# Converting the 64-bit weights of the second stage while attention runs, keeping the parts in device memory, and loading them later

## The chip, the cores and the metric

One core of one Trainium2 chip. The metric is the device time in microseconds of one execution of the whole program; lower is better. Engines are named as the profile names them: PE (TensorE), DVE (VectorE), ACT (ScalarE), POOL (GpSimd), SP (the queue that issues every DMA here).

## The reference

Three blocks in a row, each on 4 batches of 576 positions. The weights named in the kernel are `moe_w_in`, `moe_w_sg`, `moe_w_out` (first block after attention) and `moe2_w_theta`, `moe2_w_tok_r`, `moe2_w_tok_i`, `moe2_w_ch` (second block); those that are 64-bit floats come to the core as pairs of 32-bit words.

```python
# attention, 8 heads of 64 columns
scores = q @ k.T / 8 + min(-(cum_i - cum_j), 0), causal        # cum: running sum of max(s, 0)
x = softmax(scores) @ v                                        # heads side by side: 576 x 512
# first block
h = gelu(x @ w_in);  u, v = h[:, :512], h[:, 512:]
v_s = w_sg @ (layernorm(v) * g_ln) + b_sg
x = x + (u * v_s) @ w_out
# second block
theta = x @ w_theta
y = w_tok_r @ (x * cos(theta)) + w_tok_i @ (x * sin(theta))
u = x + y
out = u + max(u @ w_ch, 0)
```

## The kernel before, in words

The program is written in Python as one stream of instructions with priorities; a scheduler places each engine's instructions in an order that is fixed when the program is built. Each engine then works in that order and waits where an operand is late.

Every large product is made from operands split in two parts, a rounded one (`h`, high) and the remainder (`l`, low), with three products for each pair (high by high, high by low, low by high). A 64-bit weight is split by `split64` (L446): one ACT instruction scales the exponent word (L459, into the tile `wta`), three DVE instructions put the bits of a 32-bit float together (L460, L461, L463, on `wta` and the raw words `wraw`), an ACT cast makes the high part (L82) and a POOL subtraction the low part (L90). The same helper lines L82 and L90 serve all roundings and subtractions, and L93 all products.

The stages, in the order in which they finish:

1. Attention over 32 heads, `attention` (L411). One step g computes the scores of head g (tiles `sc`; DVE maximum L289, ACT exponential L290 into `E`), the transposes of head g-1 (L335, copied into `E0` and `Ef`), and at every second step the products `Y` with the values for a pair of heads (`pv_units`). `split_head` (L243) prepares head g+2: `qA` on POOL (L251) and DVE (L253), `kA` on ACT, `kB` on POOL, then three DMAs into `qB` and `kB`. `load_head` loads head g+4. The string `ORDER` (12 letters) or `ORDER_V` (15 letters) says in which order these pieces of a step are written.
2. Beside attention, from head 8 on, the first block of the batch just finished is fed in as filling for PE: `ffn_in` (products `fo`) and `ffn_gate` (products `fo`, result `uT`, stored as `gd`). Its 64-bit weight `w_in` is split there too (tile `wtab`), and `w_sg` is split from 32-bit floats.
3. The middle, after the last head: `ffn_in` and `ffn_gate` of batch 3; `wout` for the four batches (loads `gr` and `xr`, splits `gr` into `gh` and `gl`, products `wo`, sum `xr` at L691, store `x2d`); `theta` of batch 0 (load `x2T`, products `th`, sine and cosine). In this stage `second_weights` (L907) loads and converts `w_out`, `w_theta`, the nine slabs of `w_tok_r`/`w_tok_i` and `w_ch`: 21 slabs of 128 rows, each in two halves by `weights64` (L894), 42 pieces of 128 x 256 or 128 x 288. The call `self.later(prep)` writes one piece after every eighth unit of `ffn_in` and one after every unit of `wout`. Their raw tiles have three buffers (L899, L900).
4. The end: `mix` for batches 0 to 3 (products `yo` with `wkh`/`wkl`, products `co` with `wch`/`wcl`), with `theta` of the next batch as filling.

The tiles of the split weights (`woh`, `wol`, `wth`, `wtl`, `wkh`, `wkl`) lie where attention's tiles lay, so nothing can be written to them before attention is over. All DMAs go through the one SP queue, in order.

## Time and profile before

| | |
|---|---|
| median of 3 runs (lowest, highest) | 713.51 us (711.18 to 716.57) |
| time of the profiled execution | 712.53 us |
| its span, first to last instruction | 710.7 us |
| busy: PE, DVE, ACT, POOL | 666.2, 479.1, 378.5, 234.1 us |

Busy time is the time in which an engine has at least one instruction under way. Products overlap one another on PE, and their ends are modelled, so a PE that shows as busy is not at its peak rate; how many products pass in a stretch says more. The granted clock is a share of full speed.

Stages of the span as read from the first and last instructions of each: the first eight heads until about 69 us, heads with the first block as filling until about 363 us, the middle from 363 us until about 512 us, the end until 710.7 us.

### The profile page before, as it was taken

The numbers are of one execution on the slowest core, as the hardware profiler recorded it, in microseconds if no ns is written. First come the engines' busy times: TensorE is split into PE (matmuls) and PEld (weight loads), VectorE is DVE, ScalarE is ACT, GpSimd is POOL, SyncE is SP. The second block draws the span as 40 slices with busy tenths as digits, with TensorE's granted clock in tenths as the row PEclk, the third lists the DMA queues.
The fourth block names the chain that finished last, engine by engine and source line by source line (L and its number), as shares of the span: only waits on it lengthen the run. The fifth ranks groups of instructions, "written<-read, shape, count | busy, mean of one in ns | idle before, by whom it ended". The sixth has DMA issues, their size and how long they took to land.

```text
span 710.7 us, 12461 instructions
## 1 busy us (share of the span) xinstructions
PE 666.2 (94%) x4496; PEld 586.9 (83%) x4496; DVE 479.1 (67%) x918; ACT 378.5 (53%) x888; POOL 234.1 (33%) x257
## 2 busy tenths in 40 slices
PE   4999889999999999999999777998999999999998
PEld 3777658778979888888878667887999989989997
DVE  4788787854558565585458998898876368367522
ACT  1767556884476754668426534674744256056100
POOL 4466353464425553164237563423000100010000
PEclk9999989999999999999999899999999999999999
DMA  5665757223332344220142689973000300300101
GB/s 133 195 187 175 222 158 214 78 73 120 115 81 84 100 136 128 73 79 29 48 154 89 202 250 300 318 248 114 34 1 19 117 1 1 134 1 1 67 1 66
DMA packets 50092, 80.75 MB, mean 114 GB/s; under 512 B 7248, under 2 KB 18768, under 8 KB 50032
## 3 DMA queue, kind: packets, MB, share of 16 engines
q1 hardware_dynamic: 50032, 79.97, 36.5%
q8 instruction: 35, 0.57, 0.3%
q14 instruction: 25, 0.20, 0.1%
HBM read 56.19 MB, written 19.02 MB: 106 GB/s over the span
## 4 chain that ended last, share of the span: by engine, by line
PE 69%; DVE 9%; DMA 8%; ACT 5%; issue 3%; SPq 3%; POOL 2%; ACTq 0%; DVEq 0%; POOLq 0%
PE yo L93 16%; PE fo L93 14%; PE sc L93 8%; PE Y L93 7%; PE co L93 7%; PE th L93 6%; PE T L335 6%; PE wo L93 3%; DMA wraw<-in_moe_w_in 2%; DVE wta L461 1%; DMA gt<-in_moe_w_sg 1%; DMA x2T<-x2d 1%; ACT E L290 1%; PE tp L714 1%; DVE wta L463 1%
## 5 line engine op out<-in xcount | busy, mean ns | idle before, releaser
L290 ACT ACTIVATE E<-sc,negm 128x64 f32<-128x64 f32 (+4 forms) x160 | 84.1, 529 | 43.3 <-DVE negm L289 42.4
L289 DVE TENSOR_REDUCE negm<-sc 128x1 f32<-128x64 f32 (+4 forms) x160 | 73.8, 482 | 37.9 <-PE sc L93 36.7
L93 PE MATMUL yo<-wkh,zh 128*128 128x288 f32 x288 | 85.2, 296 | 0.1
L93 PE MATMUL yo<-wkh,zl 128*128 128x288 f32 x288 | 85.2, 297 | 0.0
L93 PE MATMUL yo<-wkl,zh 128*128 128x288 f32 x288 | 85.2, 296 | 0.0
L335 PE MATMUL T<-ident,E 128*128 128x128 f32 (+1 forms) x480 | 70.7, 278 | 1.9 <-ACT E L290 1.7
L93 PE MATMUL sc<-kA,qA 128*128 128x64 f32 (+3 forms) x192 | 64.0, 343 | 5.8 <-ACT E L290 2.5
L93 PE MATMUL sc<-kB,qB 68*128 68x64 f32 (+3 forms) x192 | 60.6, 322 | 3.8 <-DMA qB<-cpos 3.2
L335 PEld LDWEIGHTS T<-ident,E 128*128 128x128 f32 (+1 forms) x480 | 52.8, 132 | 11.3 <-ACT E L290 3.5
L86 POOL TENSOR_SCALAR xt<-x2s 128x128 fp32r<-128x128 f32 x16 | 10.9, 696 | 144.7 <-DVE x2s L90 144.7
L93 PE MATMUL fo<-x,wih 128*128 128x288 f32 x256 | 57.5, 304 | 0.2 <-ACT wih L82 0.2
L90 POOL TENSOR_TENSOR kB<-K,kA 64x576 fp32r<-64x576 f32 x32 | 50.0, 1564 | 21.0 <-ACT kA L82 18.2
L93 PEld LDWEIGHTS yo<-wkh,zh 128*128 128x128 f32 x288 | 54.0, 188 | 0.7 <-DVE x2T L787 0.4
L93 PEld LDWEIGHTS yo<-wkl,zh 128*128 128x128 f32 x288 | 54.0, 188 | 0.3
L93 PEld LDWEIGHTS yo<-wkh,zl 128*128 128x128 f32 x288 | 54.0, 188 | 0.1
L93 PE MATMUL co<-u,wch 128*128 128x288 f32 x256 | 52.9, 295 | 0.0
L93 PE MATMUL wo<-gh,woh 128*128 128x288 f32 x128 | 38.8, 305 | 10.1 <-DVE xr L691 5.6
L93 PEld LDWEIGHTS sc<-kA,qA 128*128 128x128 f32 x192 | 37.7, 200 | 11.6 <-ACT E L290 2.8
L93 PE MATMUL fo<-wih,x 128*128 128x512 f32 x128 | 44.3, 406 | 2.1 <-ACT wih L82 1.4
L93 PE MATMUL Y<-Ef,vr 128*64 128x128 f32 (+3 forms) x256 | 46.0, 467 | 0.0
L251 POOL TENSOR_SCALAR qA<-Q 128x576 fp32r<-128x576 f32 x32 | 22.4, 699 | 69.1 <-PE sc L93 54.6
L93 PEld LDWEIGHTS fo<-x,wih 128*128 128x128 f32 x256 | 42.4, 188 | 1.8 <-issue 1.2
(172 smaller groups left out, 1897.5 us busy)
## 6 DMA issues: line engine op xcount, KB each, us to landing
Q<-in_q SPq DMA_DIRECT2D x64, 144.0 KB
K<-in_k SPq DMA_DIRECT2D x64, 144.0 KB
qB<-qA SPq DMA_DIRECT2D x32, 144.0 KB
xd<-xT SPq DMA_DIRECT2D x16, 288.0 KB
gd<-uT SPq DMA_DIRECT2D x16, 288.0 KB
gr<-gd SPq DMA_DIRECT2D x16, 288.0 KB
xr<-xd SPq DMA_DIRECT2D x16, 288.0 KB
x2d<-xr SPq DMA_DIRECT2D x16, 288.0 KB
```

Of the source, the lines that this page charges most:

```text
L86: nc.gpsimd.tensor_scalar(out, src, 1.0, 1.0, op0=ALU.mult, op1=ALU.mult)
L90: e.tensor_tensor(out, a, f32(hi), op=ALU.subtract)
L93: self.nc.tensor.matmul(out, lhsT, rhs, start=start, stop=stop)
L251: nc.gpsimd.tensor_scalar(qA, Q2, 0.125, 1.0, op0=ALU.mult, op1=ALU.mult)
L289: nc.vector.tensor_reduce(negm[0:rows, col:col + 1], o, axis=ax, op=ALU.max, negate=True)
L290: nc.scalar.activation(out, o, AF.Exp, bias=negm[0:rows, col:col + 1], accum_out=sm[0:rows, j, col:col + 1])
L335: nc.tensor.transpose(T[0:n, col:col + P], E[:, c:c + n], self.ident)
L461: nc.vector.scalar_tensor_tensor(ta.bitcast(U32), Hi, 0x80000000, ta.bitcast(U32), op0=ALU.bitwise_and, op1=ALU.bitwise_or)
L463: nc.vector.scalar_tensor_tensor(ta.bitcast(U32), L, 29, ta.bitcast(U32), op0=ALU.logical_shift_right, op1=ALU.bitwise_or)
L714: nc.tensor.transpose(tp[0:r, dt * P:(dt + 1) * P], x2T[:, dt, a:a + r], self.ident)
```

## The change

The 42 pieces are no longer converted in the middle. A new generator, `convert_second`, converts them two at a time during attention: six steps for each two pieces (exponents on ACT, bits on DVE, high part on ACT, low part on POOL, store; the second piece one step behind the first), and the loads of the next two pieces at the start of the six. One step is taken at every second letter of `ORDER` or `ORDER_V`, from g = 10 on (`g > H + 1`). The high and low parts are written over the raw words and stored in `wd`, a buffer in device memory of 21 x 2 x 128 x 576 floats: 84 stores. `second_weights` now only loads them, one slab (two DMAs) at each call: 42 loads, at the same places in the program as the conversions before. To make room, `E0` and `Ef` have three buffers in place of four. `split64` is cut into `exponents64` and `bits64` with the same instructions.

```diff
-        self.E0 = [self.a1.tile([P, S], F32, name=f"E0{i}") for i in range(4)]
+        self.E0 = [self.a1.tile([P, S], F32, name=f"E0{i}") for i in range(3)]
...
-        Ef = self.a2.tile([P, 1280], F32, name="Ef", tag="Ef", bufs=4)
+        Ef = self.a2.tile([P, 1280], F32, name="Ef", tag="Ef", bufs=3)
...
-            for o in self.ORDER_V if gp > 0 and gp % 2 else self.ORDER:
+            for i, o in enumerate(self.ORDER_V if gp > 0 and gp % 2 else self.ORDER):
+                if g > H + 1 and i % 2:
+                    self.later(self.conv)
...
+            self.wd = dr.tile([21, 2, P, S], F32, name="wd")
...
+            self.conv = self.convert_second()
...
                 self.attention()
+            for _ in self.conv:
+                pass
             att.close()
...
-                self.stg = self.pool(ws, "stg", side="right")
...
+    def convert_second(self):
...
+        def load(j):
+            if j < len(pieces):
+                k, i, src, c = pieces[j]
+                raw = self.f2.tile([P, 2 * c], U32, name="wraw2", tag="wraw2", bufs=4)
+                for r, w in src:
+                    nc.sync.dma_start(raw[r:r + w.shape[0]], w[:, 2 * i * c:2 * (i + 1) * c])
+                tiles[j] = raw, self.f2.tile([P, c], F32, name="wta", tag="wta", bufs=2)
+
+        def step(j, f):
...
+            if f == "exponents":
+                self.exponents64(words, ta)
+            elif f == "bits":
+                self.bits64(words, ta)
+            elif f == "high":
+                self.rnd("act", hi, ta)
+            elif f == "low":
+                self.sub("pool", lo, ta, hi)
+            else:
+                for part, t in enumerate((hi, lo)):
+                    nc.sync.dma_start(self.wd[k, part, :, i * c:(i + 1) * c], f32(t))
+                del tiles[j]
...
+        steps = ("exponents", "bits", "high", "low", "store")
+        for j in range(0, len(pieces), 2):
+            load(j + 2)
+            load(j + 3)
+            for n in range(6):
+                if n:
+                    step(j + 1, steps[n - 1])
+                if n < 5:
+                    step(j, steps[n])
+                yield
...
     def second_weights(self):
...
+            for t in range(m):
+                for part, q in enumerate("hl"):
+                    nc.sync.dma_start(f32(getattr(self, name + q)[:, t]), self.wd[k, part, :, 0:n])
+                k += 1
+                yield
```

What this does to the order of the engines, at three places.

DVE in attention, from the preparation of one head (L253, the twentieth of 32) to that of the next. Before, only attention's own instructions stand there:

```order
L253 SCALAR_TENSOR_TENSOR qA<-Q_1939,qA 64x576
L309 TENSOR_SCALAR sm_85<-sm_85 128x10
L341 COPY Ef<-T 128x512
L310 RECIPROCAL r_86<-sm_85 128x10
L289 TENSOR_REDUCE negm_78<-sc 128x1 x2
L289 TENSOR_REDUCE negm_78<-sc_2376 128x1
L289 TENSOR_REDUCE negm_78<-sc 128x1
L337 COPY E_75<-T 64x512
L289 TENSOR_REDUCE negm_78<-sc 128x1
L253 SCALAR_TENSOR_TENSOR qA<-Q_2058,qA 64x576
```

Now, from the twentieth L253 on (L471, L472 and L474 are the three bit instructions, L460, L461 and L463 before; `wta` is the piece):

```order
L253 SCALAR_TENSOR_TENSOR qA<-Q_2076,qA 64x576
L471 TENSOR_SCALAR wta<-wta 128x288
L472 SCALAR_TENSOR_TENSOR wta<-wraw_2615,wta 128x288
L341 COPY Ef<-T 128x512
L474 SCALAR_TENSOR_TENSOR wta<-wraw_2615,wta 128x288
L309 TENSOR_SCALAR sm_85<-sm_85 128x10
L310 RECIPROCAL r_86<-sm_85 128x10
L289 TENSOR_REDUCE negm_78<-sc 128x1 x2
L471 TENSOR_SCALAR wta<-wta 128x288
L472 SCALAR_TENSOR_TENSOR wta<-wraw_2618,wta 128x288
L474 SCALAR_TENSOR_TENSOR wta<-wraw_2618,wta 128x288
L289 TENSOR_REDUCE negm_78<-sc_2577 128x1
```

Two pieces, six instructions, stand between this L253 and the third maximum. In all, 60 of the 126 bit instructions (20 pieces) stand before the twentieth L253 and 66 (22 pieces) after it, the last ahead of the twenty-eighth.

SP at the start of the middle (`gr` is the first thing that `wout` needs). Before, from the last loads of `w_out` on:

```order
L902 DMA wraw<-in_moe_w_out 128x512 x4
L902 DMA wraw<-in_moe_w_theta 128x512 x8
L902 DMA wraw<-in_moe_w_tok_r 128x576 x2
L674 DMA gr<-gd 128x576 x2
L902 DMA wraw<-in_moe_w_tok_i 128x576
L683 DMA xr<-xd 128x576 x2
L902 DMA wraw<-in_moe_w_tok_i 128x576
```

Now, at the end of the loads of the split slabs:

```order
L981 DMA wkh<-wd 128x576
L981 DMA wkl<-wd 128x576
L683 DMA gr<-gd 128x576 x2
L692 DMA xr<-xd 128x576 x3
L683 DMA gr<-gd 128x576
L675 DMA gd<-uT 128x576
```

The first `gr` stood behind 18 loads of raw pieces, which share three raw buffers; now it stands behind the 34 loads of split slabs of `w_out`, `w_theta` and `w_tok`, which wait for attention's tiles alone. The eight loads of `w_ch` come later.

DVE in the middle, around the second split of `gr` (`gl`). Before:

```order
L460 TENSOR_SCALAR wta<-wta 128x288
L461 SCALAR_TENSOR_TENSOR wta<-wraw,wta 128x288
L463 SCALAR_TENSOR_TENSOR wta<-wraw,wta 128x288
L662 SCALAR_TENSOR_TENSOR gt<-fo,gcol,bsg 128x288
L460 TENSOR_SCALAR wta<-wta 128x288
L461 SCALAR_TENSOR_TENSOR wta<-wraw,wta 128x288
L90 TENSOR_TENSOR gl<-gr,gh 128x576
L463 SCALAR_TENSOR_TENSOR wta<-wraw,wta 128x288
L662 SCALAR_TENSOR_TENSOR gt<-fo,gcol,bsg 128x288
L90 TENSOR_TENSOR gl<-gr,gh 128x576
```

Now, from the first `gl`:

```order
L671 SCALAR_TENSOR_TENSOR gt<-fo,gcol,bsg 128x288 x2
L90 TENSOR_TENSOR gl<-gr,gh 128x576 x2
L671 SCALAR_TENSOR_TENSOR gt<-fo,gcol,bsg 128x288
L90 TENSOR_TENSOR gl<-gr,gh 128x576
L671 SCALAR_TENSOR_TENSOR gt<-fo,gcol,bsg 128x288
L90 TENSOR_TENSOR gl<-gr,gh 128x576
L671 SCALAR_TENSOR_TENSOR gt<-fo,gcol,bsg 128x288
L90 TENSOR_TENSOR gl<-gr,gh 128x576
L700 TENSOR_TENSOR xr<-wo,xr 128x288 x2
L671 SCALAR_TENSOR_TENSOR gt<-fo,gcol,bsg 128x288
```

No piece is left on DVE between the gate (`gt`), the split of `gr` and the sum `xr`.

## Rows read from the trace of the kernel before

**Rows 1.** Page, part 2: busy tenths of 40 slices, 17.8 us each.

```profile
PE   4999889999999999999999777998999999999998
...
DVE  4788787854558565585458998898876368367522
```

**Rows 2.** Busy time by stage, instructions in brackets (windows of the span).

```profile
core 0: us, PE busy (x) PEld busy (x) DVE busy (x) ACT busy (x) POOL busy (x), PEclk, DMA share, GB/s
69.00:188.00 119.00, 110.51 (x707) 87.92 (x706) 82.61 (x150) 75.90 (x194) 56.44 (x55) 0.94 0.49 142
188.00:280.00 92.00, 91.97 (x641) 77.81 (x640) 57.12 (x107) 57.12 (x147) 40.35 (x45) 1.00 0.37 109
363.00:390.00 27.00, 25.70 (x152) 23.05 (x152) 22.56 (x55) 13.66 (x31) 17.50 (x20) 1.00 0.34 108
390.00:512.00 122.00, 104.13 (x660) 95.52 (x661) 107.38 (x209) 69.97 (x143) 47.32 (x52) 0.97 0.66 215
400.00:420.00 20.00, 17.60 (x118) 16.21 (x116) 19.27 (x34) 9.12 (x20) 12.50 (x13) 0.96 0.87 277
```

**Rows 3.** Chain that ended last, by line: 69-188 us, then 188-280 us.

```profile
by line: PE fo L93 19.5%; PE Y L93 12.4%; DMA wraw<-in_moe_w_in 10.4%; DMA gt<-in_moe_w_sg 8.0%; PE sc L93 6.5%; PE T L335 5.2%; ACT E L290 4.5%; issue 3.8%; DVE qA L253 2.7%; DVE negm L289 2.0%; ACT uT L640 1.8%; ACT wtab L459 1.7%; DVE wt
...
by line: PE fo L93 47.3%; PE sc L93 19.4%; PE Y L93 15.7%; PE T L335 15.2%; PE R L359 1.9%; PE sc L359 0.6%; issue 0.0%
```

**Rows 4.** Chain that ended last, middle: start, length, what.

```profile
443.23 8.80 DMA x2T<-x2d
...
455.86 0.87 PE tp L714 x8
...
498.38 3.18 PE wo L93 x24
501.56 2.73 PE th L93 x12
```

**Rows 5.** Groups of PE, 390-512 us: busy, mean | idle before.

```profile
L93 PE MATMUL wo<-gh,woh 128*128 128x288 f32 x128 | 38.8, 305 | 10.1 <-DVE xr L691 5.6 <-ACT gh L82 4.4
...
L93 PE MATMUL th<-wth,x2s 128*128 128x512 f32 x64 | 21.4, 398 | 0.9 <-DVE an L744 0.8
L93 PE MATMUL th<-wtl,x2s 128*128 128x512 f32 (+1 forms) x36 | 13.9, 391 | 0.0
...
L714 PE MATMUL tp<-ident,x2T 128*128 128x128 f32 (+1 forms) x36 | 5.1, 272 | 0.0
```

**Rows 6.** Timeline of PE, the gate of batch 3 and the first `wo`.

```profile
398.08 0.50 PE L93 MATMUL fo<-wsrh,vh 128*128 128x288 f32 x1 [3.00 <-DVE vh L90]
...
404.93 0.40 PE L93 MATMUL wo<-gh,woh 128*128 128x288 f32 x1 [0.41 <-ACT gh L82]
```

**Rows 7.** Busy time of the instructions on `wta`, by stage: DVE, ACT, POOL.

```profile
363.00:390.00 27.00, 15.48 (x32) 7.10 (x18) 6.78 (x9) 1.00 0.34 108
390.00:512.00 122.00, 48.16 (x94) 26.39 (x64) 31.65 (x34) 0.97 0.66 215
```

**Rows 8.** Timeline of SP's queue: the first `gr`.

```profile
400.46 0.90 SPq L674 DMA_DIRECT2D gr<-gd  x2
```

**Rows 9.** Timeline of DVE: the twentieth and the twenty-eighth L253.

```profile
188.33 1.85 DVE L253 SCALAR_TENSOR_TENSOR qA<-Q,qA 64x576 fp32r<-64x576 f32 x1
...
280.06 1.91 DVE L253 SCALAR_TENSOR_TENSOR qA<-Q,qA 64x576 fp32r<-64x576 f32 x1
```

**Rows 10.** Tile `wta`: durations in ns, minimum/median/maximum.

```profile
L460 DVE TENSOR_SCALAR wta<-wta x42: 272/297/915, 362.1 to 477.7; 128x256 uint32<-128x256 uint32 x24, 128x288 uint32<-128x288 uint32 x18
L461 DVE SCALAR_TENSOR_TENSOR wta<-wraw,wta x42: 396/444/1045, 363.5 to 481.0; 128x256 uint32<-128x256 uint32 x24, 128x288 uint32<-128x288 uint32 x18
L463 DVE SCALAR_TENSOR_TENSOR wta<-wraw,wta x42: 385/450/1054, 365.0 to 485.5; 128x256 uint32<-128x256 uint32 x24, 128x288 uint32<-128x288 uint32 x18
...
L90 POOL TENSOR_TENSOR wkl<-wta,wkh x18: 802/838/1803, 404.9 to 459.7; 128x288 fp32r<-128x288 f32 x18
```

**Rows 11.** Tile `qA`: DVE's subtraction, minimum/median/maximum in ns.

```profile
L253 DVE SCALAR_TENSOR_TENSOR qA<-Q,qA x32: 754/756/1973, 6.1 to 324.2; 64x576 fp32r<-64x576 f32 x32
```

More of the change, by code (lines that the diff above doesn't have):

```diff
@@ L456, in split64, with exponents64, bits64 @@
             nc.sync.dma_start(raw[0:rows].rearrange("p n t -> p (n t)"), src)
[L457 to L459 removed]
+        raw, ta = raw[0:rows], ta[0:rows]
+        self.exponents64(raw, ta)
+        self.bits64(raw, ta)
+        self.rnd("act", his, ta)
+        self.sub(sub, lo, ta, his)
+    def exponents64(self, raw, ta):
+        self.nc.scalar.mul(ta, f32(raw[:, :, 1]), 2.0 ** -112)
+    def bits64(self, raw, ta):
+        nc = self.nc
+        L, Hi = raw[:, :, 0], raw[:, :, 1]
         nc.vector.tensor_scalar(ta.bitcast(U32), ta.bitcast(U32), 3, None, op0=ALU.logical_shift_left)
@@ L818, in run @@
             self.cd = dr.tile([32, 2, S], F32, name="cd")
+            self.wd = dr.tile([21, 2, P, S], F32, name="wd")
+            rows = [slice(t * P, (t + 1) * P) for t in range(4)]
+            self.second = [([(0, w[r])], DM) for w in (self.w_out, self.w_th) for r in rows]
+            self.second += [([(0, (self.w_tr, self.w_ti)[i % 2][rows[i // 2]])], S) for i in range(8)]
+            self.second += [([(0, self.w_tr[512:576]), (64, self.w_ti[512:576])], S)]
+            self.second += [([(0, self.w_ch[r])], DM) for r in rows]
             self.cp = self.pool(root, "const")
```

52 lines of the change are left out of this document (21 added, 31 removed).

## The prediction

> **What bounds the kernel now.** I read the slices of the page first [rows 1]: PE shows nine tenths or more nearly everywhere except in slices 5 and 6 and in slices 23 to 25. In the second of these stretches DVE shows eight or nine tenths, as it does on to slice 29. So the kernel has one stage, the middle, in which PE starves beside a full DVE.
>
> Then the stages [rows 2]. From 390 to 512 us DVE is busy for 107.4 of 122 us. From 69 to 188 us (A below) it has 82.6 of 119, from 188 to 280 us (B) 57.1 of 92. A and B together leave 71.3 us of DVE unused.
>
> Third, the chains [rows 3]. In B it is products and transposes and nothing else: PE works without a pause and DVE's gaps are gaps beside it. In A the loads of `w_in` (10.4%) and `w_sg` (8.0%) are on the chain, 22 of its 119 us; there both PE and DVE wait for other things.
>
> Fourth, how much PE time the middle needs. In rows without a stall 24 `wo` products pass in 3.18 us (0.1325 each), 12 `th` products in 2.73 us (0.2275), eight transposes in 0.87 us (0.109) [rows 4]. Of the 660 PE instructions from 390 to 512 us [rows 2], 100 are `th` and 36 are `tp` [rows 5]; nearly all of the other 524 have 288 columns. 524 x 0.1325 + 100 x 0.2275 + 36 x 0.109 = 69.4 + 22.8 + 3.9 = 96.1 us. The stage takes 122, so 25.9 us are lost. The visible waits are 3.0 us for a split of `vh` [rows 6] and 10.1 us for `xr` and `gh` [rows 5]; the rest is many short ones, and products at a lower clock after the waits (granted 0.97 over the stage).
>
> **What the change removes.** From the middle go the pieces' instructions. On `wta` DVE was busy 15.5 us from 363 to 390 us and 48.2 us from 390 to 512 us [rows 7], 63.6 us for the 42 pieces but for a few instructions just before 363: 1.51 us for each piece. Without them DVE has 59.2 of 122 us left after 390. The 48 us of PE's waits and DVE's work are not the same thing, so I count the gain on PE alone: 25.9 us less what stays.
>
> What is late next? The loads. The first `gr` was issued at 400.5 us [rows 8], behind raw pieces that wait for one another's buffers, and the first `wo` product ran at 404.9 us [rows 6]. Now 34 loads of 9.4 MB stand ahead of `gr`, with nothing to wait for but attention's tiles. From 390 to 512 us the transfers ran at 215 GB/s with a share of 0.66 [rows 2], so about 326 GB/s at full share (an estimate): 9.4 MB take 29 us. Begun at about 363 us they end at 392, `gr` lands some 2 to 3 us later, and the gate's 112 products (15 us) cover PE until then. If they ran at the 277 GB/s of 400 to 420 us [rows 2], it would be 34 us and still within the gate. Over the whole stage the same bytes move as before, less those loaded ahead.
>
> Something stays: the sine chain of `theta`, the trip of `x2d` through memory into `x2T` (8.8 us on the chain [rows 4]), the round of two `gr` buffers. The nearest row is the stage from 363 to 390 us, with products in plenty and few such trips: PE misses 1.3 of 27 us [rows 2], 5%. Its bounds for 122 us are 0 and all 25.9; I take 5%, 6 us. Gain: 25.9 - 6 = 20 us (bounds 0 and 26).
>
> **What it adds to attention.** 42 pieces: 126 instructions on DVE, 84 on ACT, 42 on POOL, 46 loads and 84 stores on SP. By the order of the instructions 20 pieces stand before the twentieth L253 and 22 between it and the twenty-eighth; these run at 188 and 280 us [rows 9], so 20 fall into A and 22 into B. No work on PE.
>
> DVE price of a piece: 0.297 + 0.444 + 0.450 = 1.19 us by the medians [rows 10], 1.51 us as the crowded middle shows it. POOL also grows in attention, so I take 1.51. That is 30.3 us into A's 36.4 us of gaps and 33.3 us into B's 34.9: it nearly fits, and an engine that works in a fixed order cannot use every gap. How full can it be? The stage from 390 to 512 us shows 88%, and its fullest stretch 96% (19.27 of 20 us, 400 to 420 us [rows 2]); I take 92%. Time for A and B with a piece at p us: (139.7 + 42p) / 0.92 against 211 us now. At p = 1.51 it is 220.9, so 10 us are lost (A 4, B 6); at p = 1.19 the sum is under 211 and nothing is lost. Bounds: 0, as B's chain holds nothing but PE, and all 63.6 us.
>
> ACT gains 33.5 us [rows 7] where it was busy 133 of 211 us [rows 2], POOL 38.4 on 96.8: both stay well under DVE, cost 0. If DVE were not full, ACT at 79% would be next.
>
> Transfers: 11.6 MB of raw words in and 11.6 MB of parts out, onto 26.9 MB in A and B. Scaled by bytes, the share goes from 0.49 and 0.37 to about 0.8 in both: not full, but each transfer stands behind more. In A that touches the 22 us of loads on the chain; bounds 0 and a third more, 7 us. I take 0, because DVE's new work falls into these very waits.
>
> SP: a store waits for ACT's and POOL's part of its piece, and behind it in the queue stand the three DMAs into `qB` and `kB` of the head after next, and behind those its scores. They are queued a whole head ahead, and the eight heads of B take 92 us [rows 9], over 11 us each; a late store costs nothing until it is that late. Three buffers for `E0` and `Ef`: the fourth head back has been multiplied a step earlier in the order; 0, or short waits if `Y` runs late.
>
> **Sum.** The profiled execution took 712.5 us, 1 us under the median of 713.5. 712.5 - 20 + 10 = 702.5; I forecast 703, 1.5% under that median. A measurement of this kernel can tell about 1% from no change, 7 us.
>
> **The rivals.**
>
> *Port collisions fill DVE (slower).* `qA` on DVE takes 0.754 us alone and up to 1.973 us [rows 11], and `wta` instructions of 0.45 us up to 1.05 us [rows 10]: beside a POOL instruction a DVE instruction can stand still. Each piece brings a POOL subtraction of 0.838 us [rows 10]. If it holds up one attention instruction for half its length or a little more, 0.46 us, a piece costs 1.97 us: A and B take (139.7 + 82.7) / 0.92 = 241.7, 30.7 us more, and the total is 712.5 - 20 + 30.7 = 723. It decides from p = 1.75 on, where the loss equals the gain of 20. For it: PE's chain needs DVE's maxima, and in the new order up to six bit instructions stand in a row before one. Against it: in B the products of the first block stand between a maximum and what needs it, and keep PE fed.
>
> The Trainium skill has a rule for this: "SBUF — State Buffer", section "Who interferes with whom", says that DVE shares one pair of ports with GpSimd under an exclusive lock, that a DVE instruction with two inputs in SBUF is blocked for as long as a GpSimd instruction reads there, and that a reduction is not. The stretched `qA` agrees. By that rule taken in full every subtraction blocks a DVE instruction to its end, which puts a piece at 1.51 + 0.84 = 2.35 us, the loss at 48 us and the total at 741; by the rows alone it is 703.
>
> *The middle is held by its trips through memory (no change).* With the conversions gone, `gr` with two buffers, `xr` with three, `x2d` out and `x2T` in could still keep PE waiting for half of the 25.9 us. Gain 13, loss 10: 709. For it: 8.8 us for `x2T` on the chain [rows 4] and a share of 0.87 from 400 to 420 us [rows 2]. Against it: the 7.4 MB of `w_tok` and `w_ch` mostly leave that stretch.
>
> *Attention hides everything (faster still).* B's chain is PE alone, A waits for loads; then the loss is 0 and the total 692.5. Against it: DVE would have to run at 96% for 211 us.
>
> That the change does not do what it says can be left out: the order has the last piece ahead of the twenty-eighth of 32 heads, and none in the middle.
>
> **How the numbers follow.** Forecast 0.37, collisions 0.27, trips through memory 0.21, all hidden 0.15. The forecast's own range is 697 to 710, from 0 to 7 us for the late loads of A and 4 us to either side for the stalls that stay. About 0.72 of it lies more than 1% under the median (below 706.4), which is 0.27; with 0.15 of the hidden case and 0.03 of the third that makes 0.45 for faster. Collisions give 0.25 slower, and 0.03 comes from the edges of the others: 0.28. The rest, 0.27, is no change. The range of 8 in 10 runs from 689 (near all hidden) to 727 (collisions with a few us to spare).
>
> **What would show it.** Right: PE's loss between the start of `ffn_in` of batch 3 and the first `yo` falls to 10 us or less, the first `gr` is issued and lands before the gate ends, no `wta` stands after attention; A and B together grow by about 10 us, with DVE at 90% or more and a `wta` at about 1.5 us a piece. Wrong: attention grows by 20 us or more, with maxima late behind bit instructions and POOL subtractions, or with `w_in` late behind the new transfers; or the middle keeps more than 12 us of waits, now for `gr`, `xr` or `x2T`.

## The result, and the profile after

The changed kernel takes 717.19 us (median of 12 runs, 715.38 to 719.12) against 713.55 us (12 runs, 711.18 to 716.57). The ratio is 1.0052, with a 95% interval of 1.0037 to 1.0066: slower by half a per cent, where 1.5% faster was forecast. The range held the time, the direction was wrong.

Three places cut the span into stages: the first product of `ffn_in` of batch 3, the first product of `mix` (`yo`), and the end.

| profiled execution, us | before | after | difference |
|---|---|---|---|
| span | 710.7 | 717.4 | +6.7 |
| attention with its filling, up to the first `fo<-wih` of batch 3 | 363.6 | 391.4 | +27.7 |
| the middle, from there to the first `yo` | 145.3 | 124.1 | -21.1 |
| the end | 201.8 | 201.9 | +0.1 |

The first rows of the middle and of the end, before and then after:

```profile
363.64 0.50 PE L93 MATMUL fo<-wih,x 128*128 128x512 f32 x1 [0.68 <-DVE gt L662]
...
508.90 0.29 PE L93 MATMUL yo<-wkh,zh 128*128 128x288 f32 x1
```

```profile
391.35 0.50 PE L93 MATMUL fo<-wih,x 128*128 128x512 f32 x1 [0.68 <-DVE gt L671]
...
515.47 0.30 PE L93 MATMUL yo<-wkh,zh 128*128 128x288 f32 x1
```

The middle did what was forecast (20 us), attention lost 27.7 us where 10 were forecast. Between the medians the difference is 3.6 us and not 6.7; if the middle and the end are as in the profiles, attention lost some 25 us by the medians.

The slices of the page after, as in [rows 1] (17.9 us each):

```profile
PE   5899898798998989999999999899999999999998
...
DVE  6688898879788978676643534478686277458522
```

DVE's eights and nines, before mostly in slices 22 to 29, now stand mostly in slices 3 to 16; PE no longer has a hollow in the middle, but a seven and six eights in its first half, where it had two eights before.

The stages after, as in [rows 2] (A ended at the twentieth L253, B at the twenty-eighth; 205 and 311 us now, 188 and 280 before):

```profile
core 0: us, PE busy (x) PEld busy (x) DVE busy (x) ACT busy (x) POOL busy (x), PEclk, DMA share, GB/s
71.00:205.00 134.00, 119.15 (x723) 94.56 (x723) 111.21 (x211) 88.46 (x231) 76.28 (x75) 0.91 0.69 209
205.00:311.00 106.00, 97.16 (x631) 79.59 (x630) 87.81 (x173) 73.19 (x195) 61.62 (x67) 0.97 0.68 204
...
391.00:415.00 24.00, 23.65 (x138) 21.16 (x139) 9.84 (x27) 8.84 (x17) 8.60 (x13) 1.00 1.04 382
415.00:520.00 105.00, 101.37 (x682) 94.84 (x682) 61.03 (x113) 44.25 (x74) 11.98 (x16) 1.00 0.58 191
```

A is 133.4 us long now, 119.4 before; B 106.3, 91.7 before. DVE is busy for 111.2 of 134 us and 87.8 of 106: 83% in both, not the 92% that the sum took. PE's granted clock is lower too, 0.91 and 0.97 where it was 0.94 and 1.00 [rows 2], and PE is busy for longer with about as many products (119.2 us for 723 in A, before 110.5 for 707): a part of the loss shows as slower products between waits. From 391 to 415 us the slabs come in at 382 GB/s, more than the 326 that I had worked out, and from 415 us on DVE has 61 of 105 us to do: PE is the bound there.

The chain of waits by line, 205 to 311 us and then 311 to 389 us (the first is B; compare [rows 3]):

```profile
by line: PE fo L93 10.7%; issue 9.9%; DMA wd<-wraw 5.6%; PE sc L93 5.5%; DVE qA L253 4.7%; DMA wraw<-in_moe_w_ch 4.5%; PE Y L93 3.6%; DVE negm L289 3.6%; PE T L335 3.5%; POOL vT L570 3.5%; DVE wta L474 3.1%; DVE stats L561 2.9%; DVE wta L47
...
by line: PE fo L93 43.4%; PE sc L93 17.8%; PE Y L93 17.6%; PE T L335 16.2%; PE R L359 2.2%; POOL uT L673 1.0%; DVE gt L671 0.7%; PE sc L359 0.6%; DVE xT L387 0.5%; issue 0.5%; DVEq L387 0.0%
```

In B the chain before was PE alone. Now PE's four products make a quarter of it, and the rest is a mixture: stores of parts, raw loads of `w_ch`, `qA`, maxima, the bit instructions. From 311 us on, where no piece is left, the chain is PE alone again.

The middle after: PE's timeline at the first `wo`, then the chain around `x2T` (compare [rows 4] and [rows 6]), then SP's queue around the first `gr` (compare [rows 8]).

```profile
423.45 0.29 PE L93 MATMUL wo<-gh,woh 128*128 128x288 f32 x1
```

```profile
442.05 3.56 DMA x2d<-xr
...
447.00 5.28 DMA x2d<-xr
452.71 8.60 DMA x2T<-x2d
```

```profile
410.88 0.32 SPq L981 DMA_DIRECT2D wkl<-wd  x1
417.15 1.39 SPq L683 DMA_DIRECT2D gr<-gd  x2
```

`x2d` and `x2T` are on the chain as before (8.60 us against 8.80). The first `gr` is issued 25.8 us after the start of the stage and the first `wo` runs 32.1 us after it; before, it was 41.3 us.

### The profile page after: what moved, and what is told of

Same layout as the page of the kernel before. It is cut to its first block, busy times and chain, and to the rows that moved or that the text cites. A ratio compares the mean times of both kernels' runs of the same rounds, so it can differ in the third digit from the quotient of the medians.

```text
span 717.4 us, 12719 instructions
## 1 busy us (share of the span) xinstructions
PE 674.4 (94%) x4496; PEld 594.1 (83%) x4496; DVE 478.5 (67%) x917; ACT 376.6 (52%) x888; POOL 228.8 (32%) x257
## 4 chain that ended last, share of the span: by engine, by line
PE 55%; DVE 4%; DMA 4%; ACT 2%; issue 2%; POOL 1%; SPq 1%; ACTq 0%; DVEq 0%
PE yo L93 16%; PE fo L93 12%; PE co L93 7%; PE th L93 7%; PE wo L93 5%; PE sc L93 3%; PE Y L93 2%; PE T L335 2%; DMA x2d<-xr 1%; DMA x2T<-x2d 1%; PE tp L723 1%; DMA wd<-wraw 1%; DVE qA L253 1%; DMA wraw<-in_moe_w_ch 1%; DVE negm L289 1%
## 5 line engine op out<-in xcount | busy, mean ns | idle before, releaser
L335 PE MATMUL T<-ident,E 128*128 128x128 f32 (+1 forms) x480 | 74.4, 287 | 10.2 <-ACT E L290 5.8
L93 PE MATMUL sc<-kA,qA 128*128 128x64 f32 (+4 forms) x192 | 65.6, 354 | 11.3 <-ACT E L290 5.5
L335 PEld LDWEIGHTS T<-ident,E 128*128 128x128 f32 (+1 forms) x480 | 54.6, 137 | 20.5 <-ACT E L290 7.1
L86 POOL TENSOR_SCALAR xt<-x2s 128x128 fp32r<-128x128 f32 x16 | 9.2, 588 | 183.7 <-DVE x2s L90 183.4
L93 PE MATMUL sc<-kB,qB 68*128 68x64 f32 (+3 forms) x192 | 62.7, 333 | 3.5 <-DMA qB<-cpos 2.7
L90 POOL TENSOR_TENSOR kB<-K,kA 64x576 fp32r<-64x576 f32 x32 | 48.2, 1506 | 21.5 <-ACT kA L82 19.6
L90 POOL TENSOR_TENSOR wraw<-wta,wraw 128x256 fp32r<-128x256 f32 (+1 forms) x42 | 36.6, 877 | 40.1 <-ACT wraw L82 26.2
L93 PE MATMUL fo<-wih,x 128*128 128x512 f32 x128 | 45.8, 418 | 1.0 <-DVE gt L671 0.7
L673 POOL TENSOR_TENSOR uT<-gt,uT 128x288 f32<-128x288 f32 x32 | 27.5, 861 | 56.2 <-DVE gt L671 43.0
L93 PEld LDWEIGHTS sc<-kB,qB 68*128 68x128 f32 x192 | 40.4, 211 | 4.8 <-issue 3.0
```

The lines of the kernel that those rows point to most:

```text
L86: nc.gpsimd.tensor_scalar(out, src, 1.0, 1.0, op0=ALU.mult, op1=ALU.mult)
L90: e.tensor_tensor(out, a, f32(hi), op=ALU.subtract)
L93: self.nc.tensor.matmul(out, lhsT, rhs, start=start, stop=stop)
L335: nc.tensor.transpose(T[0:n, col:col + P], E[:, c:c + n], self.ident)
L673: nc.gpsimd.tensor_tensor(uT[:, ft, a:a + m], gt, uT[:, ft, a:a + m], op=ALU.mult)
```

## The experiments

All times in the table are read in one way: the start of batch 3 and the length of the middle from the one profiled execution, the ratio to the kernel before from the timed runs. "Against three" is the start of batch 3 less 362.1 us, that of the kernel with three buffers alone. The changed kernel contains those buffers, so that kernel is the fair base for the conversion. But a single profile can lie some us from its kernel's median: the one of *three* took 704.97 us, 3.6 under its median of 708.53, the one of *lw400_17* 4.1 over. So the column "by medians" gives the same difference from the timed runs: the ratio less that of *three*, times 713.55 us, less the difference of all that comes from the start of batch 3 on, which is taken from the profiles (it differs by little between kernels: the end is 201.8 to 202.3 us in all but *lw100*, where it is 204.7). By the intervals of the ratios it is good to 2 to 4 us either way, in *noload_nosub* and *noload_nobits* to 4 to 5. Where the two columns differ, the medians are the better measure.

| kernel | start of batch 3 | against three | by medians | middle | median | ratio to before, interval |
|---|---|---|---|---|---|---|
| before | 363.6 | +1.5 | -0.7 | 145.3 | 713.55 | 1 |
| changed | 391.4 | +29.2 | +24.1 | 124.1 | 717.19 | 1.0052, 1.0037 to 1.0066 |
| three | 362.1 | 0 | 0 | 139.1 | 708.53 | 0.9925, 0.9900 to 0.9949 |
| e03 | 356.4 | -5.7 | -7.2 | 144.9 | 706.40 | 0.9904, 0.9871 to 0.9937 |
| dmaonly | 372.1 | +10.0 | +5.7 | 123.8 | 698.61 | 0.9788, 0.9758 to 0.9818 |
| dma_late | 360.0 | -2.1 | -5.6 | 124.2 | 688.92 | 0.9636, 0.9603 to 0.9670 |
| noload | 381.6 | +19.5 | +18.0 | 123.7 | 711.34 | 0.9964, 0.9942 to 0.9986 |
| noload_nosub | 372.6 | +10.5 | +9.2 | 123.7 | 702.81 | 0.9839, 0.9780 to 0.9899 |
| noload_nobits | 367.5 | +5.4 | +1.4 | 124.7 | 696.82 | 0.9748, 0.9691 to 0.9805 |
| nobits | 374.3 | +12.2 | +11.7 | 123.8 | 704.10 | 0.9875, 0.9845 to 0.9905 |
| nosub | 378.8 | +16.7 | +14.7 | 124.4 | 706.69 | 0.9923, 0.9905 to 0.9941 |
| five | 386.3 | +24.2 | +23.8 | 123.4 | 716.20 | 1.0038, 1.0007 to 1.0068 |
| lw100 | 384.6 | +22.5 | +17.7 | 121.8 | 712.53 | 0.9969, 0.9948 to 0.9990 |
| lw400 | 384.7 | +22.6 | +21.2 | 124.5 | 713.59 | 1.0016, 0.9979 to 1.0053 |
| lw400_17 | 385.4 | +23.3 | +16.5 | 128.2 | 713.37 | 1.0006, 0.9973 to 1.0039 |
| lw400_13 | 374.7 | +12.6 | +10.0 | 131.3 | 709.92 | 0.9955, 0.9924 to 0.9986 |
| s8 | 365.3 | +3.2 | +0.9 | 137.0 | 705.58 | 0.9907, 0.9878 to 0.9937 |
| s8b | 371.9 | +9.8 | +3.8 | 137.3 | 711.43 | 0.9950, 0.9923 to 0.9977 |
| s12 | 383.0 | +20.9 | +16.5 | 130.2 | 715.75 | 1.0029, 1.0009 to 1.0050 |
| s17 | 390.0 | +27.8 | +30.0 | 127.4 | 724.83 | 1.0184, 1.0137 to 1.0230 |

The middle is 123.4 to 124.7 us in every kernel with all 42 pieces in attention at the scheduler's old priorities: that term does not depend on how the pieces are made. All the rest is attention.

The ratios show the same ranking as the starts of batch 3 for the kernels that have all 42 pieces in attention.

### Which theories there were

L: ACT and DVE stand, in their fixed order, before pieces whose raw words are late. D: DVE's time for the bit instructions. C: POOL's subtractions hold DVE up. T: the new transfers make attention's own loads late. The first four kernels take one thing away each.

**nobits**: `self.bits64(words, ta)` replaced by `pass`.

> The changed kernel without the three DVE bit instructions of each piece (126 instructions; the parts that are stored and later multiplied are then not the weights' values). Exponents, high part, low part, loads and stores stay. Before: first block of batch 3 starts at 364 us, total 713.5; changed: 391 us, total 717. Theory L (late loads: in the fixed order ACT and DVE stand before a piece whose raw words have not landed, and the maxima and exponentials behind them are late): ACT still waits for the raw words, only DVE no longer does, so about half of the 27.7 us stays: start of batch 3 at 376 to 382, total 702 to 708. Theory D (the DVE time of the bit instructions itself, at less than the 92% that I assumed): nearly all of the loss goes: 364 to 368, total 690 to 694. Theory C (collisions with POOL's subtractions): the subtractions stay and hit attention's own DVE instructions, most of the loss stays: 385 or later, total 711 or more.

**noload**:

```diff
-                for r, w in src:
-                    nc.sync.dma_start(raw[r:r + w.shape[0]], w[:, 2 * i * c:2 * (i + 1) * c])
...
+        one = self.a2.tile([P, 576], U32, name="one", tag="one", bufs=1)
+        nc.sync.dma_start(one, self.w_out[0:P, 0:576])
...
-            words = raw.rearrange("p (n t) -> p n t", t=2)
+            words = one[:, 0:2 * c].rearrange("p (n t) -> p n t", t=2)
```

> The changed kernel in which the 42 raw pieces are not loaded: one raw tile is loaded once and every piece is computed from it into its own rotating tile and stored (so the parts are not those of the weights). All ACT, DVE and POOL instructions, and the stores, stay. Theory L (ACT and DVE wait for raw words that come late): 15 to 25 of the 27.7 us go, start of batch 3 at 367 to 376, total 693 to 702. Theory D (the DVE time itself) and theory C (collisions with POOL): no wait that counts is removed, start at 386 or later, total 712 to 717. Theory T (the extra transfers delay attention's own loads) would put half of the gain here, as half of the bytes go: 378, total 704.

**dmaonly**: only the branch `store` of `step` is left, its source a tile of zeros.

> The changed kernel with the transfers alone: the 46 raw loads and 84 stores of the conversion stand where they stood, but no ACT, DVE or POOL instruction converts anything; the stores take a tile of zeros (so the second part multiplies by zeros). Theory T (the transfers themselves delay attention's own loads): 10 to 28 us of the loss stay, start of batch 3 at 374 or later, total 700 or more. Theories L, D and C: nothing stands on ACT and DVE, the loss goes but for a few us: start at 363 to 368, total 689 to 694.

**five**:

```diff
-tag="wraw2", bufs=4)
+tag="wraw2", bufs=5)
...
             load(j + 2)
-            load(j + 3)
             for n in range(6):
+                if n == 2:
+                    load(j + 3)
```

`wta` also moves to another pool (`a2` in place of `f2`).

> The changed kernel with five raw tiles in place of four, and the load of the second piece of the next pair issued two steps later, so that each load takes a tile whose store was issued four steps or more before (in the changed kernel one of the two takes a tile whose store was issued one step before). Nothing else changes. Theory L: the waits of ACT for raw words and of DVE for ACT go for the most part: start of batch 3 at 372 to 382, total 698 to 708. Theories D and C: no change, 388 to 393, total 715 to 718.

Measured: batch 3 starts at 374.3, 381.6, 372.1 and 386.3 us. Not one theory holds alone. The transfers alone cost 10.0 us against *three* (5.7 by the medians), the work without raw loads costs 19.5 (18.0), and the two add up to about the 29.2 (24.1) of the changed kernel, though the 84 stores are in both. Without the bits 17 us go (12.4), more than without the raw loads (9.7, or 6.1) and much less than all, as D had it. L, which the chain in B had put first, is weak: with a fifth tile the waits of the bit instructions for ACT almost halve, as the waits after (the changed kernel, then *five*; engine and line, what it waited for, us in total, times, longest) show, but the median moves by 1 us.

```profile
DVE wta L471 <- ACT wta L466: 17.4, 11, 5.5
...
ACT wta L466 <- DMA wraw<-in_moe_w_ch: 8.9, 5, 5.3
```

```profile
DVE wta L471 <- ACT wta L466: 9.7, 10, 3.5
```

The work alone, *noload*, is slow without any raw load to wait for: its busy time by stage, and its chain in B by line:

```profile
core 0: us, PE busy (x) PEld busy (x) DVE busy (x) ACT busy (x) POOL busy (x), PEclk, DMA share, GB/s
71.00:196.30 125.30, 111.58 (x707) 90.26 (x704) 116.68 (x215) 89.93 (x236) 80.30 (x77) 0.95 0.61 179
196.30:300.70 104.40, 95.78 (x638) 79.40 (x637) 89.57 (x168) 70.85 (x187) 60.03 (x66) 0.98 0.50 155
```

```profile
by line: PE fo L93 14.3%; PE sc L93 8.3%; DVE wta L474 6.2%; DVE qA L253 6.2%; PE Y L93 6.1%; DVE wta L471 5.5%; DVE wta L472 5.5%; PE T L335 4.9%; issue 4.4%; DVE vl L90 4.0%; DVE negm L289 3.9%; DMA wd<-wraw 3.6%; ACT E L290 3.1%; DMA xd<
```

DVE is at 93% in A and 86% in B, and the three bit instructions take 17% of B's chain. No raw word can be late there, and 19.5 us (18.0) are lost all the same.

### The transfers: where they stand

**dma_late**: the transfers alone once more, with `g > H + 8` in place of `g > H + 1`, and the tile of zeros written first from the `qA` just prepared, so that no store can be moved ahead of that.

> Transfers alone, as in the kernel with nothing else, but begun only behind the loads of w_in and w_sg in the SP queue. Theory T (the 10 us are w_in and w_sg, late behind the raw loads): attention as in the kernel with three buffers, batch 3 at 361 to 365, total 687 to 692. If the bytes themselves slow attention's own loads: 370 or more, total 697 or more.

Measured: 360.0 us, 2.1 us earlier than *three* (5.6 by the medians): the same loads and stores cost nothing. (The loads are 44, not 46 as in the prediction: 42 pieces, and one slab of two sources adds two.) The edit did less than the expectation says: not all raw loads stand behind `w_sg` now. SP's queue shows what moved: the first raw loads and the last loads of `w_sg`, in the changed kernel, in *dmaonly* and in *dma_late* (a row gives the start of its first load; x4 is four in a row):

```profile
86.19 1.92 SPq L926 DMA_DIRECT2D wraw<-in_moe_w_out  x4
...
162.02 1.11 SPq L519 DMA_DIRECT2D gt<-in_moe_w_sg  x2
```

```profile
86.02 1.92 SPq L926 DMA_DIRECT2D wraw<-in_moe_w_out  x4
...
160.07 1.87 SPq L519 DMA_DIRECT2D gt<-in_moe_w_sg  x2
```

```profile
104.36 2.02 SPq L927 DMA_DIRECT2D wraw<-in_moe_w_out  x3
...
133.13 4.64 SPq L520 DMA_DIRECT2D gt<-in_moe_w_sg  x4
```

In *three* the very last `w_sg` is issued at 129.9 us. In the changed kernel it is 162.5, in *dmaonly* 160.6, in *dma_late* 137.2. Ahead of it stand 13 raw loads and 21 stores in the changed kernel, 14 and 24 in *dmaonly*, 14 and none in *dma_late*, whose first raw load also comes 18 us later. Between *dmaonly* and *dma_late* lie 1.5% of the time, some 11 us. So it is where the stores and the first raw loads stand, among `w_in` and `w_sg`, and not the number of bytes, that costs the 10 us (5.7); which of the two costs more was not tried.

That they cost it by way of the late `w_sg` is likely and not shown. In *noload_nobits* 36 stores and no raw load stand ahead of the last `w_sg`, it is issued at 154.3 us, and with ACT's and POOL's work on top only 5.4 us are lost (1.4, by an interval of some 4 either way).

### The work: bits, subtractions, ACT

**noload_nobits** is *noload* without the bit instructions, **noload_nosub** is *noload* without POOL's subtractions, **nosub** the changed kernel without them. In the last two the store loop reads `enumerate((hi, hi))` in place of `(hi, lo)`.

> The changed kernel without the raw loads (one raw tile, loaded once) and without the three DVE bit instructions (so the parts are not the weights'). ACT's 84 instructions, POOL's 42 subtractions and the 84 stores stay. Theory W (the second part of the loss is DVE's own time): against the kernel with three buffers (batch 3 at 362 us) attention loses 0 to 6 us, total 688 to 695. If ACT and POOL cost by themselves (exponentials and head preparations behind the pieces): 8 us or more, start at 370 or later, total 697 or more.

> The changed kernel without raw loads and without POOL's subtractions (the high part is stored twice); ACT and DVE instructions and stores stay. The kernel without raw loads starts batch 3 at 381.6 us. Theory C (the subtractions stretch DVE instructions): the mean of a bit instruction falls, DVE is busy for 6 to 10 us less in attention, and the start moves by 6 to 12 us: 370 to 376, total 698 to 704. If they only lengthen the way to the stores: 379 to 382, total 708 to 711.

> The changed kernel without the 42 POOL subtractions in attention: the high part is stored twice (so the low parts of the second stage's weights are wrong by that). ACT, DVE and all transfers stay. Theory C (DVE stands still beside POOL's subtractions; the rival that I priced at 0.46 us for each piece, 19 us): start of batch 3 at 370 to 378, total 697 to 705, and the bit instructions get shorter. Theories D and L (DVE's own time, and raw words that come late): 385 to 391, total 711 to 717.

Measured: 367.5, 372.6 and 378.8 us. With neither raw loads nor bits, ACT, POOL and the stores cost 5.4 us by themselves, 1.4 by the medians, which is not clear of nothing. Taking away the 42 subtractions gives back 9.0 us without raw loads and 12.6 with them (8.8 and 9.4 by the medians), against 19 for the rival as I had priced it. One place where it comes from is seen on DVE, in the groups of *noload* and then of *noload_nosub* (71 to 311 us; busy, mean ns of one | idle before):

```profile
L472 DVE SCALAR_TENSOR_TENSOR wta<-one,wta 128x256 uint32<-128x256 uint32 x24 | 17.9, 760 | 0.2
...
L471 DVE TENSOR_SCALAR wta<-wta 128x256 uint32<-128x256 uint32 x24 | 13.0, 553 | 1.0 <-ACT wta L466 0.9
L474 DVE SCALAR_TENSOR_TENSOR wta<-one,wta 128x256 uint32<-128x256 uint32 x24 | 13.0, 549 | 0.2
```

```profile
L472 DVE SCALAR_TENSOR_TENSOR wta<-one,wta 128x256 uint32<-128x256 uint32 x24 | 15.5, 660 | 0.2
...
L474 DVE SCALAR_TENSOR_TENSOR wta<-one,wta 128x256 uint32<-128x256 uint32 x24 | 13.4, 568 | 0.2
...
L471 DVE TENSOR_SCALAR wta<-wta 128x256 uint32<-128x256 uint32 x24 | 8.2, 356 | 1.0 <-ACT wta L466 0.8
```

Beside subtractions the first bit instruction takes 553 ns on average, without them 356, and the second 760 against 660; the third shows no such difference (549 and 568). The busy time on `wta` is 74.4 us in *noload* and 63.1 in *noload_nosub*: 1.77 and 1.50 us for a piece. Over the whole span DVE's busy time falls from 489.0 to 471.2 us, 0.42 us for each subtraction; in the changed kernel against *nosub* it is 478.5 against 471.9, 0.16 us for each. The price that I took from the middle, 1.51 us, is here that of a piece without a subtraction beside it. And *noload_nosub*, where that price holds, loses 10.5 us (9.2): the forecast's 10. Without its subtractions POOL is also busy for 36 us less in A and B (140.3 us in *noload*, 104.3 here), and the stores need not wait for them; how much of the 9 us comes that way, and not by way of DVE, the runs do not tell.

The rule of the Trainium skill that I had weighed ("SBUF — State Buffer", section "Who interferes with whom": DVE and GpSimd share a pair of ports under an exclusive lock) is right in kind. The timeline of the changed kernel, POOL and then DVE, has a pure case:

```profile
96.03 1.40 POOL L90 TENSOR_TENSOR kB<-K,kA 64x576 fp32r<-64x576 f32 x1 [0.72 <-ACT kA L82]
97.40 1.26 POOL L90 TENSOR_TENSOR wil<-wtab,wih 128x512 fp32r<-128x512 f32 x1
...
96.05 3.23 DVE L253 SCALAR_TENSOR_TENSOR qA<-Q,qA 64x576 fp32r<-64x576 f32 x1
```

`qA` on DVE, 0.754 us alone, begins with a POOL instruction under way and ends 0.6 us after the second of two that follow each other without a gap: 3.23 us. Taken in full for every subtraction, as I had done for a rival, the rule would give 0.84 us a piece; the runs show 0.16 to 0.42. In the changed kernel 6 of the 42 subtractions begin with DVE idle and 8 during a maximum; why the average is so low was not worked out further.

### The buffers, and the order

**three**:

```diff
-        self.E0 = [self.a1.tile([P, S], F32, name=f"E0{i}") for i in range(4)]
+        self.E0 = [self.a1.tile([P, S], F32, name=f"E0{i}") for i in range(3)]
...
-        E0 = self.E0[g % 4]
-        Ef = self.a2.tile([P, 1280], F32, name="Ef", tag="Ef", bufs=4)
+        E0 = self.E0[g % 3]
+        Ef = self.a2.tile([P, 1280], F32, name="Ef", tag="Ef", bufs=3)
```

> The kernel before with one part of the change alone: E0 and Ef with three buffers in place of four; no weight is converted earlier. Theories L, D, C and T: no difference, start of batch 3 at 363 to 365, total 712.5 to 714.5. Theory B (the fourth buffer was in use, and what waits for it is part of the loss): 2 to 8 us later, total 716 or more.

Measured: no theory had this. The part that I had put at 0 makes the kernel faster by 0.75%. SP's queue and DVE's timeline of *three*:

```profile
103.59 1.61 SPq L902 DMA_DIRECT2D wraw<-in_moe_w_out  x3
...
129.34 1.10 SPq L510 DMA_DIRECT2D gt<-in_moe_w_sg  x2
...
113.16 0.48 DVE L460 TENSOR_SCALAR wta<-wta 128x256 uint32<-128x256 uint32 x2
...
114.17 0.74 DVE L461 SCALAR_TENSOR_TENSOR wta<-wraw,wta 128x256 uint32<-128x256 uint32 x2
```

In the middle of attention three raw pieces of `w_out` are loaded and put together (nine bit instructions in all; the casts follow at 353 us). My reading is that their staging tiles lie in memory that attention no longer takes, so the scheduler may place them wherever DVE has room. Six raw pieces are loaded early in all. DVE's work from the start of batch 3 to the first `yo` falls from 126.3 to 120.3 us, and the middle falls with it, from 145.3 to 139.1. Attention itself is as long as before (1.5 us shorter in the profile, 0.7 longer by the medians).

**e03** has the E0 lines of that diff and not the Ef lines.

> The kernel before with E0 in three buffers and Ef still in four. The kernel with both in three was 4.4 us faster than before; its trace shows three pieces of w_out converted at 113 to 120 us, since the staging tiles lie in memory that no tile of attention takes any more. Theory M (the freed memory does it, not another order of the instructions): E0 alone frees less (2.3 KB of the 7.3 KB in a partition), the pieces stay behind attention, total 712 to 715. Theory O (the other order of the instructions does it): E0 alone brings most of the reordering, total 707 to 710.

Measured: both theories are half right. No piece is converted before 354 us and the middle is as long as before (144.9), so the 6 us of the middle in *three* go with the three pieces done early. But attention ends 7.2 us earlier than before (6.5 by the medians), with the same instructions in another order: I take it that one buffer less gave the scheduler another order, and that another order alone is worth some 7 us. Nothing else was changed, but the order of this kernel was not varied by itself, and the granted clock from 69 us to the twentieth L253 differs too, 0.97 here and 0.94 before.

**lw100** and **lw400** give the conversion in the complete changed kernel a lower priority for the scheduler (`LATER_W` 100 and 400 in place of 0).

> The changed kernel with the conversion's instructions at a lower priority for the scheduler (by 100 places); the same instructions, in another order (949 lines of difference on DVE). Theory W with T (work and transfers cost what they cost): batch 3 at 386 to 396, total 712 to 722. If the order that the scheduler happened to find made most of the loss: 380 or less, total 706 or less.

> The complete changed kernel with the conversion at a priority lower by 400 places. Now 4 raw loads stand ahead of the last load of w_in in the SP queue and 12 ahead of the last of w_sg (16 and 33 in the changed kernel, 11 and 26 with 100 places); all 42 pieces stand between the fifteenth and the twenty-ninth preparation of a head. Theory T with W: most of the transfers' 10 us go and the work's 19.5 us stay, batch 3 at 380 to 385, total 706 to 712. If denser work costs more than the transfers give back: 387 or more, total 714 or more.

Measured: 384.6 and 384.7 us, ratios 0.9969 and 1.0016: by these 6 and 3 us less than the changed kernel (the 3 are not clear of the noise), and level with the kernel before or slightly better. The counts in the second text are of the conversion's loads and stores together; in its trace 6 raw loads and 8 stores are issued ahead of the last `w_sg`, at 138.7 us. In *lw100* that is at 152.2, and *lw100* is no slower. So the few us that come back cannot be put down to the transfers alone, and most of the loss (22 us; 18 and 21 by the medians) stays.

### How many pieces attention can take

If idle DVE time were what counts, a few pieces would fit at no cost. Six kernels convert the first 8, 12, 13 or 17 slabs in attention (`self.second[:8]` and so on) and the rest in the middle as before; `wraw2` and `wta` lie in pool `a2` there. In *s8*, *s8b*, *s12* and *s17* a DVE copy of one element from the `qA` just prepared into the raw tile keeps the scheduler from moving a load far ahead of where it is written.

> Only the first 8 of the 21 slabs (w_out and w_theta, 16 pieces) are converted in attention, at half the pace (a pair of pieces in two heads, each pair's loads held back by a tiny DVE copy from the head just prepared); the other 13 slabs are converted in the middle as in the kernel before. Theory D (DVE is filled beyond what a fixed order can use): the loss grows faster than the number of pieces, because 16 pieces (24 us of DVE) fit into the gaps: attention loses 2 to 7 us, the middle still gains 10 to 16: total 700 to 708. Theory L (each late load costs by itself): the slower pace gives loads time, loss 0 to 4, total 698 to 705. If loss and gain are both in proportion to the pieces (27.7 and 21.2 us times 16/42, or 10.6 and 8.1): 716.

> 17 of the 21 slabs (all but w_ch, 34 pieces) are converted in attention at the pace of the changed kernel, with the same tiny copies; the four slabs of w_ch are converted in the middle. Theory D: DVE in A and B is still close to full, attention loses 16 to 22 us, the middle gains 18 to 21: total 709 to 716. Proportional: loss 22.4, gain 17.2: total 718.7.

> As the kernel with 8 slabs in attention, but begun nine heads later (from g = 19, a third of the letters): w_in and w_sg have long been loaded and converted by then. Theory T (part of the loss is that w_in and w_sg come late behind the new transfers, up to 10 us as the kernel with transfers alone shows) with theory D (16 pieces fit into DVE's gaps): attention ends within 2 us of the kernel with three buffers alone, batch 3 starts at 361 to 365, middle 137, total 703 to 707. If A's loss has nothing to do with w_in, the pieces cost as much here: 366 to 370, total 708 to 712.

> 12 slabs (24 pieces) converted in attention, from g = 15 at a third of the letters, gated in the same way; nine slabs in the middle. Theory D: the pieces (40 us of DVE at 1.67 us) go into B and the heads after it, where 61 us of gaps are left; attention loses 4 to 9 us against the kernel with three buffers, the middle gains 4 to 8: total 704 to 711. In proportion to the changed kernel (29 us times 24/42 lost, 15 times 24/42 gained): 717.

> As the kernel with 400 places, with 17 slabs (34 pieces) in attention and w_ch in the middle. Theory W: against the same with 21 slabs attention gains 3 to 6 us (8 pieces at 0.46 us) and the middle loses 2 to 5: total within 3 us of it. If the last pieces cost most: 4 us less or better.

> As the kernel with 400 places, with 13 slabs (26 pieces) in attention. Theory W: against the same with 21 slabs attention gains 7 to 10 us, the middle loses 5 to 9: total within 4 us of it. If the middle can take 16 pieces at almost no loss, as DVE has room there: 5 us less or better.

Measured: *s8* is the best of the versions that convert early, 0.9907 of the kernel before; it loses 3.2 us in attention against *three* for 16 pieces (0.9 by the medians) and gains 2.2 in the middle, so against *three* it is no clear gain. *s8b*, with the same 16 pieces where DVE has most room and `w_in` is long done, starts batch 3 9.8 us later in the profile; by the medians it loses 3.8 us, give or take 2.6, or 0.24 us for each piece, and DVE is busy there for 72 of 101 us:

```profile
183.90:284.70 100.80, 94.94 (x646) 80.02 (x645) 72.22 (x154) 65.74 (x174) 51.23 (x56) 0.98 0.54 163
```

```profile
ACT wta L467 <- DMA wraw<-in_moe_w_theta: 9.6, 7, 3.3
...
ACT wta L467 <- DMA wraw<-in_moe_w_out: 5.8, 3, 2.9
```

(The waits are those of 184 to 334 us.) So DVE's idle share does not say what a piece costs: at 72% a piece of *s8b* costs 0.24 us by the medians, one of *noload_nosub*, with DVE at 87% in A and B, 0.22. ACT, which makes the exponentials, stood 15.4 us before raw words in *s8b*; in *s8* these two waits are 12.5 us (110 to 334 us), so they do not set the two apart. *s17* came out slower than both of its forecasts, *s12* near the one in proportion (717); they pay 0.87 and 0.82 us for a piece (0.69 and 0.88 by the medians), more than the changed kernel (0.70, or 0.57). Without the copies, *lw400_13* pays 0.48 (0.39) for each of 26 pieces. *lw400_17* and *lw400* end attention at the same time in the profiles, with 34 and 42 pieces; by the medians they lose 16.5 and 21.2 us, half a microsecond for each piece in both. That the cost of a piece is set by what stands behind it on ACT and DVE when it is late, and so by the order, is how I read this; only *lw100* and *lw400* change the order alone, by 6 and 3 us.

## Why the prediction was wrong, step by step

- **The middle, gain 20 us.** Right as a sum (21.1), and PE's loss there is down to 25.9 - 21.1 = 4.8 us, under the 10 asked for (its rows from 391 to 520 us show 4.0 us of idle time). Three buffers alone, which I had put at 0, take 6.1 us off the middle by letting three pieces go early; against that kernel the conversion brings 15.0 (139.1 to 124.1).
- **What is late next in the middle.** Right: the last of the 34 loads was issued at 410.9 us, 20 us after the start of the stage, and PE had no wait ahead of the first `wo`. The rival of the trips through memory falls: `x2T` is on the chain as before, and the stage is short.
- **A and B, loss 10 us: the step that failed.** It measured 27.7, or 29.2 against the kernel with the same buffers (24.1 by the medians). Two terms of the sum make the difference. (a) *"I take 0" for the late loads in A*: the transfers alone cost 10.0 us (5.7). The bound was 7, because I scaled the two loads' time on the chain by bytes; in the runs it is their place that costs, as the same transfers later in the queue cost nothing (*dma_late*): in SP's one queue the stores and raw loads put the last load of `w_sg` back by 33 us. (b) *"At p = 1.51"*, the price read in the middle, holds in attention only without subtractions: the 42 of them add 9.0 us (8.8), for which the sum had no term. ACT, POOL and the stores, put at 0, cost 5.4 us by themselves in the profile but 1.4 by the medians, which is within the noise; with the bits at my price they make the 10.5 us (9.2) of *noload_nosub*. 10.5 + 9.0 + 10.0 = 29.5 us, against 29.2 measured; by the medians 9.2 + 8.8 + 5.7 = 23.7, against 24.1. That this closes so well is partly luck, as the stores are in the first and the last term and a new order alone seems able to move attention by 7 us.
- **DVE at 92%.** In the complete kernel this divisor is what failed, more than DVE's work. DVE's busy time in A and B is 199.0 us, no more than the 139.7 + 63.4 = 203.1 of the sum; at 92% it would have fitted into 216 us, and it took 240: waits, and not a DVE that the pieces had filled up, took the rest. DVE's share is 83% in the changed kernel, 90% with raw words at hand (206.3 of 229.7 us), and in *noload_nosub* 92% in the first 119 us of A:

```profile
71.00:190.00 119.00, 106.17 (x691) 87.10 (x688) 109.90 (x222) 88.68 (x233) 60.00 (x54) 0.96 0.64 194
190.00:290.00 100.00, 94.59 (x648) 79.42 (x647) 80.83 (x161) 71.80 (x187) 44.29 (x46) 0.98 0.51 154
```

- **The rival of the collisions (0.27).** It named the end (slower) and one of the two mechanisms; its 19 us were 9.0 to 12.6 (about 9 by the medians), and DVE did not fill up by it. The price of a piece in the changed kernel, 68.5 us of DVE on `wta` for 42 pieces, is 1.63 us: under the 1.75 from which I let it decide. What stands in DVE's groups there, as in [rows 10], is stretched pieces and waits for ACT (idle before L471):

```profile
L474 DVE SCALAR_TENSOR_TENSOR wta<-wraw,wta 128x256 uint32<-128x256 uint32 x24 | 13.9, 588 | 0.1
L472 DVE SCALAR_TENSOR_TENSOR wta<-wraw,wta 128x256 uint32<-128x256 uint32 x24 | 13.2, 551 | 0.2
...
L471 DVE TENSOR_SCALAR wta<-wta 128x256 uint32<-128x256 uint32 x24 | 11.1, 464 | 10.0 <-ACT wta L466 9.8
...
L471 DVE TENSOR_SCALAR wta<-wta 128x288 uint32<-128x288 uint32 x18 | 8.8, 486 | 7.8 <-ACT wta L466 7.6
```

- **SP's queue, "a late store costs nothing until it is that late".** Wrong for the first gate's weights, which were not queued a head ahead but piece by piece among the new transfers. (As under (a): that these cost the time is likely, not shown.)
- **Three buffers: 0.** Wrong in sign: they make the kernel faster by 0.75%.

Open: how much of the loss is the order that the scheduler happened to find, and how much is PE's lower granted clock in A and B. *lw100* and *lw400* show 3 to 6 us of order and transfers together; a good order for the whole conversion may exist, and was not found.

## What to carry to other kernels

Work moved from a full stage into "gaps" can cost time that the gaps' length does not show: here 24 us or more, with DVE idle for 17% of the stage. Before moving it, look for the loads that the new transfers will stand in front of (here those of `w_in` and `w_sg`), and put the new ones behind them. Take the price of an instruction from rows where its neighbours are those it will have. Compare kernels by their medians before reading a few microseconds out of single profiles. Test each part of a change by itself, the "free" ones first: here the free part, one buffer less, was the whole gain worth having, and the part that the change was made for cost more than it brought.

## What was not expected of the hardware

A two-operand DVE instruction took 3.23 us in place of 0.754 beside two POOL instructions in a row. The one-operand shift L471 took 553 ns on average beside POOL's subtractions in *noload* and 356 without them in *noload_nosub* (pieces of 256 columns). That is not a rule yet: in the changed kernel the same instruction took 464 ns with the subtractions, and in *nosub* 508 without. The loads of the split slabs ran at 382 GB/s from 391 to 415 us, where the stretch from 400 to 420 us had shown 277 before [rows 2].
